# Retention followed by a gated feed-forward on one core: the sums of w_out as ScalarE negations plus accumulating transfers from GpSimd

## The chip, the cores and the metric

The kernel runs on one core of a Trainium2 chip. The metric is device time in microseconds; lower is better. The time before is 667.25 us, the median of three runs (667.02 to 668.68). The profiled execution took 667.05 us, of which 665.3 us are the span that the profile shows. TensorE's granted clock was 0.999 of full speed.

The engines are named as in the profile: PE is TensorE's matmuls and PEld its weight loads, DVE is VectorE, ACT is ScalarE, POOL is GpSimd, SP is SyncE, from whose queue the kernel's transfers start.

## The reference

```python
# retention: q, k, v are (4, 8, 768, 64)
for t in range(S):
    state = gamma[None, :, None, None] * state + np.einsum('bhd,bhe->bhde', k[:, :, t], v[:, :, t])
    y[:, :, t] = scale * np.einsum('bhd,bhde->bhe', q[:, :, t], state)
# to (3072, 512) tokens x, then the feed-forward; w_in is (512, 2048), w_out (2048, 512)
h = x @ w_in
sp = np.maximum(h, 0.0) + np.log1p(np.exp(-np.abs(h)))     # softplus
g = h * erf(sp)
return (g @ w_out).astype(np.float32)
```

The retention part produces the tokens 128 at a time (a chunk `j`); the feed-forward, which is nearly all of TensorE's work, consumes them.

## The kernel before

**Tokens and groups.** The first 512 tokens go through the feed-forward with plain matrix products, in groups 0 to 3 of 512 hidden features each (`hidden`, `project`). From group `G0` = 4 on, a group is 256 tokens times one half `s` of the hidden features (1024 of them); group 4 is half 0 of tokens 512 to 767, group 5 half 1 of the same tokens, group 6 half 0 of the next 256 tokens, and so on to group 23. "The first later group" of the change is group 5.

**Products from sums.** From group 4 on, the second product of the feed-forward is computed in 2x2 blocks with seven block products instead of eight, by a Strassen-Winograd scheme (`PRODUCTS`, `project_part`). It needs four sums of w_out blocks for each half: `T1 = 12 - 11`, `T2 = 22 - T1`, `T4 = 21 - T2`, `T3 = 22 - 12`, where "11", "12", "21", "22" are blocks of w_out. They are made once in the kernel by `sums(s)` and stay in `w_out_sb`; T3 is written over block "12", which the plain products of groups 0 and 1 must have read. Products 1, 2 and 3 need a plain block of w_out, 4 needs T4, 5 needs T1, 6 needs T2 and 7 needs T3. The first product (`hidden_steps`) uses a larger scheme of 26 steps on 4x4 blocks, with 30 sums of w_in for each half (`W_SUMS`, made by `sum_in(s, upto)`), from group 5 on. Group 4 still makes its hidden values with eight plain products (`hidden_plain`), since w_in's sums for half 0 overwrite plain blocks that group 4 uses.

**Order.** The order on each engine is written out by hand: a statement's place in the Python text is its place in its engine's queue, and each engine works its queue strictly in order. Generators are used to place small pieces: `next(last_steps)` emits the next sum of w_out (first the four of half 0, then the four of half 1), `w_sums` one sum of w_in of half 0, `e_sums` one sum of gated activations, `next_chunk` one step of the preparation of the next chunk of q and k. The dictionary `order` tells after which of the 26 hidden steps which of these are placed.

**A later group `g`.** In turn: 26 hidden steps, each one product into PSUM (L950) and one or two evictions, by DVE (L962, adding into h) or, for the first write to a block of h, by ScalarE (L964, L966); among them, at steps 14, 18 and 24, the products 1, 2 and 4 of the group before (L1033). Then ScalarE's softplus (L816), the retention visit (`sub_visit`), ScalarE's erf (L829), and the products 5, 6, 7 and 3 of the group before. DVE then multiplies h with erf (`gated`, L848). After an odd group DVE also makes the sums of the tokens for the next two groups (`x_sums`, L932). The hidden steps need w_in's sums, and the products 4 to 7 need the sums of w_out for the half of the group before.

**Where the sums stand before.** In group 4: 30 sums of w_in for half 1 on DVE, the four sums of w_out for half 0 (two before `project(3, 0)`, two after erf), then 8 sums of w_in for half 0. In group 5: the other 22 sums of w_in for half 0 (two each after steps 1 to 4, nine among steps 14 to 24, five after the visit). In group 6: three sums of w_out for half 1, after steps 12, 15 and 22, and the fourth after the visit.

**PSUM buffers of group 4.** Each of the eight plain products of `hidden_plain` goes into one of two "hp" buffers and is copied out by ScalarE (L982), so product n + 2 waits for copy n.

**Transfers.** All large transfers of this part start from SP: per chunk 256 KB each of k and v, 16 + 16 small ones of 16 KB for q and k in blocks (`load`), and the stores of the output, 256 KB each. GpSimd's queue is empty after the constants at the start.

Of the kernel before, what the change touches and what calls it, by code (L numbers as in the profile page):

```python
# [15 lines left out]
AF = mybir.ActivationFunctionType  # L16
ALU = mybir.AluOpType
# [28 lines left out]
W_SUMS = (  # L46
    (16, 2, 6, "+"),
    (17, 8, 10, "-"),
    (4, 4, 17, "+"),
    (10, 10, 16, "+"),  # L50
    (18, 16, 4, "-"),
    (19, 18, 5, "-"),
    (20, 1, 19, "-"),
    (20, 0, 20, "+"),
# [82 lines left out]
def kernel(  # L137
# [13 lines left out]
    nc = tc.nc  # L151
# [73 lines left out]
    def w_in_of(ft, kk):  # L225
        half, s, i = ft // (2 * FG), ft % (2 * FG) // FG, ft % FG
        return w_in_sb[:, s, 4 * (2 * half + i // 2) + kk, i % 2 * P : (i % 2 + 1) * P]
# [112 lines left out]
    def sum_in(s, upto):  # L340

        assert all(("hidden", 2 * FG + s * FG + u) in done for u in range(FG))
        for to, a, b, sign in W_SUMS[in_sums[s] : upto]:
            nc.vector.tensor_tensor(w_in_sb[:, s, to], w_in_sb[:, s, a], w_in_sb[:, s, b], op=OP[sign])
        in_sums[s] = max(in_sums[s], upto)

    def sums(s):

        assert ("project", s) in done
        x = {name: w_out_sb[:, s, at] for name, at in OUT.items()}  # L350
        for to, a, b in (("T1", "12", "11"), ("T2", "22", "T1"), ("T4", "21", "T2"), ("T3", "22", "12")):
            nc.vector.tensor_tensor(x[to], x[a], x[b], op=ALU.subtract)  # L352
            done.add((to, s))
            yield

# [15 lines left out]
    def later_sums():  # L371
        for s in range(2):
            yield from sums(s)

    weight_steps = weights()
    last_steps = later_sums()
# [155 lines left out]
    def prepared(j):  # L532

        if j >= NJ:
            return
        nc.vector.tensor_tensor(
            KQ[j][:, 0], KQ[j][:, 0],
            kq_s[:, j % NC, 0, :, None].to_broadcast([P, H, D]), op=ALU.mult,
        )
        yield  # L540
        blocks = (KB[j], KQ[j][:, 1].rearrange("p h d -> p (h d)"))
        for i, x in enumerate(blocks):
            x = x.rearrange("p (u a d) -> p u a d", u=HP, d=32)
            by = kq_b[:, j % NC, i, :, :, None].to_broadcast([P, HP, 4, 32])
            nc.vector.tensor_tensor(x, x, by, op=ALU.mult)
            yield
        for name, store, x in zip("kq", (KT, QT), blocks):
            store[j] = ret.tile([P, HP, C], F32, name=name + "T")
            nc.vector.transpose(store[j].rearrange("p u t -> p (u t)"), x)
            yield  # L550
# [156 lines left out]
    def sub_begin(j, pool=None):  # L707
        SC[j] = [ret_psum(pool) for _ in range(2)]
        sub_scores(j)
        sub_additions(j)  # L710
# [100 lines left out]
    def gate_softplus(g):  # L811


        name = "r" if g < 4 and g % 2 else "e"
        E[g] = act.tile([P, N], F32, name=name, bufs=1)
        nc.scalar.activation(E[g], HS[g], AF.Softplus)  # L816
# [28 lines left out]
    def gated(g, part=None):  # L845
        for a in range(2) if part is None else (part,):
            half = slice(a * N // 2, (a + 1) * N // 2)
            nc.vector.tensor_tensor(E[g][:, half], HS[g][:, half], E[g][:, half], op=ALU.mult)  # L848
            pace(-1.1)
# [61 lines left out]
    G0 = n_ft // FG  # L911
# [5 lines left out]
    def chunk_of(g):  # L917
        return TCH // SCH + (g - G0) // 2
# [51 lines left out]
    def hidden_plain(g):  # L970

        m, s = chunk_of(g), (g - G0) % 2
        HS[g] = act.tile([P, N], F32, name="h")
        h = HS[g].rearrange("p (f t u c) -> p f u t c", f=2, t=2, u=FG)
        x = XC[m // 2][:, :, m % 2 * SCH : (m % 2 + 1) * SCH]
        for f, u in itertools.product(range(2), range(FG)):
            to = ps_h.tile([P, TCH], F32, name="hp")[:, :SCH]
            for kk in range(n_k):
                nc.tensor.matmul(  # L979
                    to, w_in_of((2 * f + s) * FG + u, kk), x[:, kk], start=kk == 0, stop=kk == n_k - 1  # L980
                )
            nc.scalar.copy(h[:, f, u], to.rearrange("p (t c) -> p t c", t=2))  # L982
            yield
        done.update(("hidden", (2 * f + s) * FG + u) for f in range(2) for u in range(FG))
# [62 lines left out]
    def put_part(m, step):  # L1047


        o26, o57, o34, o1 = (O[m][i] for i in range(4))  # L1050
        if step == 0:
            R[m] = act.tile([P, 8, DH], F32, name="r", bufs=1)
            nc.scalar.copy(R[m][:, 7], o1[:, 0])
            return
        r = R[m]
        t0 = m * SCH
        if step == 1:
            nc.vector.tensor_tensor(
                r[:, 0:5:4], o26, r[:, 7:8].to_broadcast([P, 2, DH]), op=ALU.add
            )  # L1060
        elif step == 2:
            nc.vector.tensor_tensor(
                r[:, 5:7], o57, r[:, 4:5].to_broadcast([P, 2, DH]), op=ALU.add
            )
            nc.vector.tensor_tensor(r[:, 3], r[:, 6], o57[:, 0], op=ALU.add)
        else:
            nc.vector.tensor_tensor(r[:, 1:3], r[:, 5:7], o34, op=ALU.add)
            for t in range(2):
                nc.sync.dma_start(
                    out[t0 + t * P : t0 + (t + 1) * P, :],  # L1070
                    r[:, 2 * t : 2 * t + 2].rearrange("p a c -> p (a c)"),
                )
# [103 lines left out]
    def all_of(steps):  # L1176
        for _ in steps:
            pass
# [9 lines left out]
    load(j + 2)  # L1188
    gated(G0 - 1)
    for n, _ in enumerate(hidden_plain(G0), start=1):  # L1190
        if n == 3:
            sub_begin(j)
    sum_in(1, 20)
    x_sums(G0)
    sub_states(j)
    all_of(prepared(j + 1))
    next(last_steps)
    next(last_steps)
    sum_in(1, len(W_SUMS))
    project(G0 - 1, 0)  # L1200
    nc.scalar.activation(idle, idle, AF.Softplus)
# [3 lines left out]
    put_first(0)  # L1205
    gate_erf(G0)
    next(last_steps)
    next(last_steps)
    for tt in range(1, TT):
        project(G0 - 1, tt)  # L1210
        put_first(tt)
    gated(G0)
    sum_in(0, 8)
    j += 1

    def sums_left():
        for n in range(9, len(W_SUMS) + 1):
            sum_in(0, n)
            yield

    w_sums = sums_left()
    put = None
    for g in range(G0 + 1, NG):
        even = (g - G0) % 2 == 0
        more = j < NJ
        if put is not None:
            put_part(put, 0)
        e_sums = g_sums(g - 1)
        next(e_sums)
        next_chunk = prepared(j + 1) if even or put is None else iter(())  # L1230

        if put is not None:
            order = {18: (e_sums,), 20: (e_sums,), 24: (e_sums, e_sums)}
        else:
            order = {
                10: (next_chunk,), 14: (next_chunk, e_sums), 16: (next_chunk, e_sums),
                18: (next_chunk, e_sums), 20: (e_sums,), 24: (next_chunk,),
            }
        if g == G0 + 1:
            order.update({n: (w_sums,) * 2 for n in (1, 2, 3, 4)})  # L1240
            order[14] += (w_sums, w_sums)
            order[16] += (w_sums,)
            order[18] += (w_sums, w_sums)
            order[20] += (w_sums, w_sums)
            order[24] += (e_sums, w_sums, w_sums)
        elif g == G0 + 2:
            order.update({n: (last_steps,) for n in (12, 15, 22)})
        for n, _ in enumerate(hidden_steps(g), start=1):
            if put is not None and n in (14, 16, 18):
                put_part(put, n // 2 - 6)  # L1250
            for steps in order.get(n, ()):
                next(steps, None)
            if n in (14, 18, 24):
                project_part(g - 1, {14: 1, 18: 2, 24: 4}[n])
        put = None
        all_of(e_sums)
        all_of(next_chunk)

        nc.scalar.activation(idle, idle, AF.Softplus)
        gate_softplus(g)  # L1260
        if more:
            sub_visit(j, g)
        all_of(w_sums)
        if g == G0 + 2:
            all_of(last_steps)
        if g + 1 < NG and not even:
            x_sums(g + 1)
        if more:
            if even:
                all_of(prepared(j + 2))  # L1270
            if j + 3 < NJ:
                load(j + 3)
            j += 1
        gate_erf(g)
        for p in (5, 6, 7, 3):
            project_part(g - 1, p)
        if even:
            put = chunk_of(g - 1)
        if g == NG - 1:
            last_gated(g)  # L1280
        else:
            gated(g)

    g, m = NG - 1, chunk_of(NG - 1)
# [57 lines left out]
```

## Time and profile before

| engine | busy us | share of the span | instructions |
|---|---|---|---|
| PE | 657.3 | 99% | 6200 |
| PEld | 557.2 | 84% | 6200 |
| DVE | 517.0 | 78% | 1109 |
| ACT | 272.4 | 41% | 394 |
| POOL | 4.6 | 1% | 21 |

The costs of what the change touches, from the groups of the trace:

| what | line, engine | count | us each |
|---|---|---|---|
| sum of w_out, 128x1024 f32 | L352, DVE | 8 | 1.22 |
| sum of w_in, 128x256 f32 | L344, DVE | 60 | 0.42 |
| copy of a plain hidden product, 128x256 | L982, ACT | 8 | 0.37 |
| softplus or erf, 128x2048 | L816, L829, ACT | 22 + 21 | 1.91 |
| loading of an activation table | ACT | several a group | 1.28 |

How to read it: a share of busy time is a mean over the whole span. PE at 99% has few idle places, and a change that moves work between other engines can save only what PE idles there; so the table tells what moves, and the stretches of the trace, group by group, tell where it matters. An instruction's "idle before" with a releaser names the engine whose signal ended the wait. ACT's idle time of 128 us before softplus, for example, ends with DVE's last eviction and is only the rhythm of the groups.

The trace places group 4's plain products at 127.67 to 142.9 us, group 5's first hidden step at 158.48 and group 6's at 185.14.

### The profile page before, as it was taken

The numbers are of one execution on the slowest core, as the hardware profiler recorded it, in microseconds if no ns is written. First come the engines' busy times: TensorE is split into PE (matmuls) and PEld (weight loads), VectorE is DVE, ScalarE is ACT, GpSimd is POOL, SyncE is SP. The second block draws the span as 40 slices with busy tenths as digits, with TensorE's granted clock in tenths as the row PEclk, the third lists the DMA queues.
The fourth block names the chain that finished last, engine by engine and source line by source line (L and its number), as shares of the span: only waits on it lengthen the run. The fifth ranks groups of instructions, "written<-read, shape, count | busy, mean of one in ns | idle before, by whom it ended". The sixth has DMA issues, their size and how long they took to land.

```text
span 665.3 us, 15218 instructions
## 1 busy us (share of the span) xinstructions
PE 657.3 (99%) x6200; PEld 557.2 (84%) x6200; DVE 517.0 (78%) x1109; ACT 272.4 (41%) x394; POOL 4.6 (1%) x21
## 2 busy tenths in 40 slices
PE   8999999999999999999999999999999999999998
PEld 7744444576888999999999999999999999999997
DVE  5999999988997788678678678777787688476464
ACT  3468364344424244244244343442442542533440
POOL 1000000100000000000000000000000000000000
PEclk9999999999999999999999999999999999999999
DMA  9999944333421222222322322231232210000000
GB/s 188 222 241 216 236 133 106 63 62 61 116 41 32 66 49 45 70 42 48 73 40 46 73 41 45 36 77 34 47 79 36 43 55 1 2 33 0 1 33 32
DMA packets 158261, 47.68 MB, mean 72 GB/s; under 512 B 143088, under 2 KB 149616, under 8 KB 158192
## 3 DMA queue, kind: packets, MB, share of 16 engines
q1 hardware_dynamic: 157776, 46.72, 32.5%
q8 instruction: 48, 0.79, 0.5%
q14 instruction: 21, 0.17, 0.1%
q10 hardware_dynamic: 416, 0.01, 0.0%
HBM read 40.39 MB, written 6.29 MB: 70 GB/s over the span
## 4 chain that ended last, share of the span: by engine, by line
PE 95%; DVE 3%; DMA 1%; issue 1%; SPq 0%; ACT 0%; DVEq 0%
PE o L1033 36%; PE hp L950 21%; PE r L950 11%; PE hp L859 8%; PE o L895 8%; PE hp L979 2%; PE r L735 2%; PE hp L627 1%; PE o L771 1%; DVE h L962 1%; DMA kq<-in_k_dram 1%; PE r L556 1%; PE o L603 1%; PE r L750 1%; PE hp L750 1%
## 5 line engine op out<-in xcount | busy, mean ns | idle before, releaser
L1033 PE MATMUL o<-w_out_sb,h 128*128 128x256 f32 (+1 forms) x648 | 143.8, 379 | 0.4 <-DVE r L1297 0.4
L950 PE MATMUL hp<-xs,w_in_sb 128*128 128x128 f32 x988 | 138.9, 275 | 0.6 <-DVE h L962 0.6
L1033 PEld LDWEIGHTS o<-w_out_sb,h 128*128 128x128 f32 x648 | 120.5, 190 | 17.1 <-DVE r L1297 0.6
L950 PEld LDWEIGHTS hp<-xs,w_in_sb 128*128 128x128 f32 x988 | 128.3, 192 | 4.7 <-DVE h L962 1.8
L962 DVE TENSOR_TENSOR h<-h,hp 128x256 f32<-128x256 f32 x190 | 77.7, 418 | 67.5 <-PE hp L950 62.8
L1033 PE MATMUL o<-w_out_sb,e 128*128 128x256 f32 x480 | 113.6, 380 | 1.6 <-DVE w_out_sb L352 1.6
L1033 PEld LDWEIGHTS o<-w_out_sb,e 128*128 128x128 f32 x480 | 86.8, 190 | 11.2 <-DVE w_out_sb L352 1.8
L816 ACT ACTIVATE e<-h 128x2048 f32<-128x2048 f32 x22 | 42.0, 1911 | 128.0 <-DVE h L962 128.0
L962 DVE TENSOR_TENSOR h<-h,r 128x256 f32<-128x256 f32 x152 | 56.9, 415 | 21.6 <-PE r L950 20.7
L964 ACT COPY h<-hp 128x256 f32<-128x256 f32 x38 | 14.1, 372 | 132.7 <-PE hp L950 116.6
L950 PE MATMUL r<-xs,w_in_sb 128*128 128x128 f32 x456 | 63.3, 275 | 0.0
L950 PEld LDWEIGHTS r<-xs,w_in_sb 128*128 128x128 f32 x456 | 57.0, 192 | 0.0
L859 PE MATMUL hp<-xT,w_in_sb 128*128 128x512 f32 (+2 forms) x144 | 56.5, 548 | 0.0
L848 DVE TENSOR_TENSOR e<-h,e 128x1024 f32<-128x1024 f32 x42 | 49.3, 1214 | 9.2 <-ACT e L829 9.2
L859 PEld LDWEIGHTS hp<-xT,w_in_sb 128*128 128x128 f32 x144 | 25.8, 190 | 27.0 <-issue 24.6
L950 PE MATMUL hp<-xT,w_in_sb 128*128 128x128 f32 x304 | 46.3, 275 | 0.0
L950 PEld LDWEIGHTS hp<-xT,w_in_sb 128*128 128x128 f32 x304 | 41.5, 192 | 1.4 <-issue 0.5
L829 ACT ACTIVATE e<-e 128x2048 f32<-128x2048 f32 (+1 forms) x23 | 42.1, 1836 | 0.2
L966 ACT ACTIVATE h<-hp 128x256 f32<-128x256 f32 x57 | 21.8, 383 | 29.8 <-PE hp L950 28.5
L950 PE MATMUL r<-xT,w_in_sb 128*128 128x128 f32 x228 | 31.7, 275 | 0.0
L829 ACT ACT_TABLE_LOAD x24 | 30.8, 1283 | 0.4
L950 PEld LDWEIGHTS r<-xT,w_in_sb 128*128 128x128 f32 x228 | 28.5, 192 | 0.0
(159 smaller groups left out, 789.8 us busy)
## 6 DMA issues: line engine op xcount, KB each, us to landing
w_out_sb<-in_moe_w_out_dram SPq DMA_DIRECT2D x14, 512.0 KB, 6.6
kq<-in_k_dram SPq DMA_DIRECT2D x23, 256.0 KB, 4.0
v<-in_v_dram SPq DMA_DIRECT2D x23, 256.0 KB, 3.2
out_dram<-r SPq DMA_DIRECT2D x23, 256.0 KB, 2.6
kq<-in_q_dram SPq DMA_DIRECT2D x288, 16.0 KB, 1.8
kb<-in_k_dram SPq DMA_DIRECT2D x288, 16.0 KB, 1.7
w_in_sb<-in_moe_w_in_dram SPq DMA_DIRECT2D x8, 512.0 KB, 12.6
w_in_sb<-in_moe_w_in_dram SPq DMA_DIRECT2D x8, 256.0 KB, 8.0
```

Of the source, the lines that this page charges most:

```text
L735: nc.tensor.matmul(pp[r][col * D : (col + 1) * D, u % 2, t], x[own, u, :], QT[j][own, u, t], start=first(r, col), stop=True, skip_group_ch ...
L750: nc.tensor.matmul(other[a][own, u % 2, D:] if crossed else pp[a][own, u % 2, t], V[j][t, 2 * u + r, :], AM[j][t, r, u, :D], start=crossed ...
L816: nc.scalar.activation(E[g], HS[g], AF.Softplus)
L829: nc.scalar.activation(E[g][:, half], E[g][:, half], AF.Erf)
L848: nc.vector.tensor_tensor(E[g][:, half], HS[g][:, half], E[g][:, half], op=ALU.mult)
L859: nc.tensor.matmul(HP_[ft][:, t], w_in_of(ft, kk), XC[0][:, kk, t], start=(kk == 0), stop=(kk == n_k - 1),)
L895: nc.tensor.matmul(O[0][tt].rearrange("p (d c) -> p d c", d=2), E[g][:, u * TCH + tt * P : u * TCH + (tt + 1) * P], w_out_of(ft), start=(f ...
L950: nc.tensor.matmul(to[:, u, :], w_in_sb[:, s, w, u * P : (u + 1) * P], XS[m](x), start=first and u == 0, stop=True, skip_group_check=True,)
L962: nc.vector.tensor_tensor(h, h, of, op=ALU.add if plus else ALU.subtract)
L964: nc.scalar.copy(h, of)
L966: nc.scalar.activation(h, of, AF.Copy, scale=-1.0)
L1033: nc.tensor.matmul(O[m][i][:, half, at], G[g][a][:, u * P : (u + 1) * P], w_out_sb[:, s, OUT[b], u, at], start=i not in started, stop=(s = ...
```

## The change

Each sum of w_out is made in two parts instead of one DVE instruction: ScalarE writes the negated second operand to the sum's place (an activation Copy with scale -1), and a transfer from GpSimd's queue adds the first operand to it while it writes (128 partitions x 4 KB, 512 KB). The order of the four becomes T1, T2, T3, T4. T2 is computed from T1 and T4 from T2, so ScalarE's negation of T1 waits for T1's transfer, and that of T2 for T2's. T3 is negated in place over block "12", so after T1's transfer has read it.

The places change as well. Half 0: T1, T2 and T3 after plain products 1, 4 and 7 of group 4, T4 after erf of group 4. Half 1: T1, T2 and T3 after hidden steps 11, 17 and 23 of group 5, T4 after the visit of group 5, ahead of its erf; none is left in group 6. Of w_in's sums for half 0, 12 now stand before gating in group 4 and 8 after it (8 after it before), and 10 are left for group 5 (one each after steps 1 to 4, 14, 16, 18, 20 and 24, and one after the visit). The aim is to take work off DVE in the groups around the switch to the sums.

```diff
-        for to, a, b in (("T1", "12", "11"), ("T2", "22", "T1"), ("T4", "21", "T2"), ("T3", "22", "12")):
-            nc.vector.tensor_tensor(x[to], x[a], x[b], op=ALU.subtract)
+        for to, a, b in (("T1", "12", "11"), ("T2", "22", "T1"), ("T3", "22", "12"), ("T4", "21", "T2")):
+            nc.scalar.activation(x[to], x[b], AF.Copy, scale=-1.0)
+            nc.gpsimd.dma_start(x[to], x[a], accum_op=ALU.add)
             done.add((to, s))
             yield
...
     for n, _ in enumerate(hidden_plain(G0), start=1):
+        if n in (1, 4, 7):
+            next(last_steps)
         if n == 3:
             sub_begin(j)
     sum_in(1, 20)
     x_sums(G0)
     sub_states(j)
     all_of(prepared(j + 1))
-    next(last_steps)
-    next(last_steps)
     sum_in(1, len(W_SUMS))
     project(G0 - 1, 0)
...
     gate_erf(G0)
     next(last_steps)
-    next(last_steps)
+    sum_in(0, 12)
     for tt in range(1, TT):
         project(G0 - 1, tt)
         put_first(tt)
     gated(G0)
-    sum_in(0, 8)
+    sum_in(0, 20)
     j += 1
 
     def sums_left():
-        for n in range(9, len(W_SUMS) + 1):
+        for n in range(21, len(W_SUMS) + 1):
...
         if g == G0 + 1:
-            order.update({n: (w_sums,) * 2 for n in (1, 2, 3, 4)})
-            order[14] += (w_sums, w_sums)
-            order[16] += (w_sums,)
-            order[18] += (w_sums, w_sums)
-            order[20] += (w_sums, w_sums)
-            order[24] += (e_sums, w_sums, w_sums)
-        elif g == G0 + 2:
-            order.update({n: (last_steps,) for n in (12, 15, 22)})
+            order.update({n: (w_sums,) for n in (1, 2, 3, 4)})
+            for n in (14, 16, 18, 20, 24):
+                order[n] += (w_sums,)
+            order.update({n: (last_steps,) for n in (11, 17, 23)})
...
         all_of(w_sums)
-        if g == G0 + 2:
+        if g == G0 + 1:
             all_of(last_steps)
```

## The prediction

> **What bounds the kernel now.** I read the page first (busy shares, then the chain that ended last), then the tile and line of the sums that the change moves, then a table of stretches around the groups it touches, then the waits inside one of them.
>
> The shares and the head of the chain:
>
> ```profile
> PE 657.3 (99%) x6200; PEld 557.2 (84%) x6200; DVE 517.0 (78%) x1109; ACT 272.4 (41%) x394; POOL 4.6 (1%) x21
> ...
> PE 95%; DVE 3%; DMA 1%; issue 1%; SPq 0%; ACT 0%; DVEq 0%
> ```
>
> TensorE is the bound; only the places where it stands still can be won. The change touches DVE, ACT and POOL, so I looked for TensorE's idle time in the groups concerned. In the next view each line is one stretch: its bounds, its length, then busy time per engine. I cut from the first to the last matmul of the seven-product steps (L950, with the three L1033 products placed among them) of groups 5, 6, 7 and 8, and between these the 32 matmuls of the products 5, 6, 7, 3:
>
> ```profile
> 127.67:158.48 30.81, 30.81 (x242) 20.81 (x241) 26.53 (x64) 11.72 (x19) 0.00 (x0) 1.00 0.35 64
> 158.48:178.20 19.72, 19.34 (x258) 18.16 (x256) 17.93 (x46) 6.20 (x12) 0.00 (x0) 1.00 0.40 92
> 178.20:185.14 6.94, 6.94 (x33) 6.11 (x34) 6.35 (x25) 4.42 (x5) 0.00 (x0) 1.00 0.35 66
> 185.14:207.13 21.99, 20.16 (x258) 18.38 (x256) 19.01 (x38) 5.97 (x11) 0.00 (x0) 1.00 0.15 28
> 207.13:214.07 6.94, 6.94 (x33) 6.12 (x33) 6.78 (x13) 4.42 (x6) 0.00 (x0) 1.00 0.33 63
> 214.07:233.05 18.98, 18.98 (x258) 18.17 (x256) 13.34 (x29) 5.97 (x11) 0.00 (x0) 1.00 0.26 62
> ...
> 240.00:258.97 18.97, 18.97 (x258) 18.16 (x256) 13.78 (x30) 5.97 (x11) 0.00 (x0) 1.00 0.17 32
> ```
>
> The same 258 matmuls take 18.98 us in groups 7 and 8, where DVE is busy for 13.3 to 13.8, but 19.72 in group 5 (DVE 17.9) and 21.99 in group 6 (DVE 19.0). So **0.74 us in group 5 and 3.01 us in group 6** are lost because DVE is late; group 4 (the first line) has no idle TensorE at all. The waits inside group 6 name the cause, the w_out sums of L352, and that line's own answer gives their length:
>
> ```profile
> PEld o L1033 <- DVE w_out_sb L352: 1.8, 1, 1.8
> PE o L1033 <- DVE w_out_sb L352: 1.6, 1, 1.6
> PEld hp L950 <- DVE h L962: 1.0, 3, 0.4
> ...
> L352 DVE TENSOR_TENSOR w_out_sb<-w_out_sb x8: 1182/1216/1224, 140.0 to 208.7; 128x1024 f32<-128x1024 f32 x8
> ```
>
> The product 4 waited 1.6 us for its T4, the third such sum; the rest of the 3.01 us is small waits for evictions queued on DVE behind the sums.
>
> **What the Trainium skill says.** "DMA: Bandwidth & Descriptors", section "SWDGE vs HWDGE vs iDMA": accumulating in a transfer goes only by GpSimd's software path. Its section "Anatomy of one DMA — SWDGE (gpsimd) path" prices a transfer of that path at 2.0 us + bytes/436e3; for 512 KB that is 3.2 us, and its "Rules for kernel authors" say that an accumulate reads its destination and writes it later, so a second stream is read. The trace of before has no such transfer. "SBUF — State Buffer", section "Who interferes with whom": DVE's tensor_tensor with both inputs in SBUF takes GpSimd's read interface only, and descriptor generation needs the write interface (inferred, by that page), so DVE's sums should not starve it. No run here shows that yet. ScalarE's price needs no page; the trace has the shape:
>
> ```profile
> L314 ACT ACTIVATE w_out_sb<-w_out_sb,below 128x1024 uint32<-128x1024 uint32 x7 | 8.0, 1149 | 8.1 <-DVE w_out_sb L313 8.1
> L829 ACT ACTIVATE e<-e 128x1024 f32<-128x1024 f32 x2 | 2.0, 1049 | 0.0
> ```
>
> **The change part by part.**
>
> DVE loses eight L352 sums, 8 x 1.216 = 9.7 us. Four lay in group 4, where TensorE has no idle time: worth nothing. Three lay inside group 6's stretch (3 x 1.22 = 3.65 us) and one right after it. Without them group 6's DVE time falls from 19.0 to 15.4. Further, DVE enters group 6 earlier: of the 5 w_in sums before the sums of x one remains, 4 x 0.41 = 1.6 us, so gating of group 5 (2.35 us at 186.04) falls earlier by that much and part of it leaves the stretch: about 13.8, which is group 8's load, and group 8 has no idle. **Gain 3.0 us.**
>
> The w_in sums of half 0: before, 8 in group 4 and 22 in group 5; now 20 and 10. In group 4 DVE starts them at 149.15, where the w_out sums stood: 12 x 0.387 = 4.65 us to 153.8, ScalarE's erf having ended at 152.6; gating 2.36 to 156.2; 8 + 4 more sums, 4.65 us, to 160.8. The first eviction on DVE started at 161.03 before, so nothing is late: cost nothing, hidden behind the 24 matmuls of L895 (10.6 us) and the first steps that ScalarE evicts. In group 5 four sums fewer stand among steps 14 to 24 (9 before, 5 now): 4 x 0.41 = 1.6 us off an engine that made TensorE lose 0.74. **Gain 0.7 us.**
>
> ScalarE gains eight negations of 128x1024. I take 1.05 us each (the f32 row; the other row is 1.15). Eight are 8.4 us on an engine busy for 41%. Three stand between the copies of group 4's plain product; a copy takes 0.37 and comes every 1.72 us, so 1.42 fits. One stands after erf of group 4, before copies that wait up to 2.9 us for TensorE. The other four are in group 5. By duration alone they cost nothing.
>
> The waits are the new thing. T2 is computed from T1, T4 from T2, so ScalarE's negation for T2 waits until T1's transfer has landed, and what follows on ScalarE's queue waits too. Call **L** the time from the end of a negation to the landing of its transfer, as seen by a waiting engine.
> - Group 4, half 0. T1's negation ends at 129.97 + 1.05 = 131.0. T2's stands behind the fourth copy (ends at 136.43). Copy 5 must begin by 138.8, since step 7 begins at 139.2 in the buffer that copy 5 frees (two buffers). So T1 must land by 137.8: **L up to 6.8 costs nothing**, each further us costs one.
> - Group 5, half 1. T1's negation follows the copy that ends at 163.52, and ends at 164.57. T2's ends at 165.62 + L (for L over 3.3), T3's one later, then ScalarE loads the softplus table for 176.2: in time up to L = 8. T2's sum lands at 165.62 + 2L. T4's negation waits for that, behind the copies to xT that end at 178.7; behind it stand the erf table (1.28) and erf (1.91), and for erf waits DVE's gating, free for it at 183.7. 183.7 - 1.91 - 1.28 - 1.05 = 179.5, so **L up to 6.9 costs nothing**; beyond, erf slips by 2 us for each us. Some 1.6 us of slip are free, because before gating ended 3.25 us into group 6 and the first TensorE wait there came only after the L352 sum at 191.8.
> - TensorE's matmuls of products 4 to 7 now wait for transfers. Half 0's last (T4, negated by 153.7) lands near 160 and is first read at 173.3; half 1's lands near 186 and is read at 199. Nothing.
>
> How long is L? Lower end: 3.2 us, the page's price. With the second stream read at the same rate (1.2 us more) 4.4. Upper end: 512 KB loads of w_out took 6.6 us in the trace, at a time when the engines were 90% busy; with 1.2 us for a second read 7.8, and a slow adder could make it 10. The engines are 20 to 40% busy around 131 to 138 and 163 to 173, mostly with 16 KB loads, and a 256 KB store lands in 3.4 us there. I take **L = 5.5 us**, under both limits.
>
> Other loads: the accumulating transfers share the engines with the kb loads of group 4, for which DVE idled 0.76 us at 137.5. A further us there is hidden, as DVE has 2.4 us less to do before its mask at 147.96.
>
> Sum: 667.25 - 3.0 - 0.7 = **663.5 us**. The rest of the span (the groups after 6, at 18.98 or less with TensorE full, and the head) does not change.
>
> **The rivals.**
> 1. *The transfer's latency takes the place of the sums.* At L = 10: group 4 loses 10 - 6.8 = 3.2; group 5's erf slips 2 x 3.1 = 6.2, less 1.6 free, 4.6. So 663.5 + 3.2 + 4.6 = **671.3 us**, slower. For it: two limits within 1.5 us of my L, an unseen transfer kind, ScalarE strictly in order. Against it: the 3.4 us stores and the page's 3.2 us. It breaks even near L = 8.6.
> 2. *Half of it comes.* L between 7 and 8.5, or DVE starving descriptor generation now and then (DVE is busy for 4.97 of the 5 us from 163 to 168). At L = 8: 1.2 + 0.6 = 1.8 lost, **665.3 us**; near 8.5 no change.
> 3. *DVE stays late in group 6 because gating and the sums of x bind it, not L352.* Then only the 1.6 us wait goes: **665.6 us**. Against it: groups 7 and 8 have gating too and no idle.
>
> **How the numbers follow.** Forecast 0.68, slow transfer 0.18, rivals 2 and 3 together 0.14 (half of these gain over 2.0 us, which is 0.3%; most of the rest are within it). Faster 0.73, within 0.3% 0.09, slower 0.18. The range starts at 662.9 (all 3.75 us, and a little drift) and reaches over rivals 2 and 3 into the weakest third of rival 1: 668.5. Inside are 0.68 + 0.14 + 0.05.
>
> **What would show it.** Right: group 6's 258 matmuls in 19.0 us and group 5's in under 19.2, no TensorE wait on DVE's w_out_sb, no idle TensorE in group 4, ScalarE waiting under 1 us for w_out_sb's transfers at the second negation of group 4. Wrong: ScalarE's copies L982 late behind a wait for a transfer; erf of group 5 ending after 184.5; transfers over 7 us from issue to landing.

## The result, and the profile after

The changed kernel takes **663.28 us**, the median of four runs (663.08 to 663.55), against 667.36 us for the kernel before, measured beside it. The ratio is 0.9936, with a 95% interval of 0.9918 to 0.9953. Measured again beside two of the experiments it was 663.14 us, ratio 0.9930 (0.9918 to 0.9942). The forecast was 663.5 us. About a third of the runs of the kernel before, and fewer or none of most others, take 1.5 to 2 us longer than the rest, so a ratio and the medians shown beside it can differ by up to 0.2%.

The page of the changed kernel begins its shares and its chain like this (busy time and share of each engine, then the share of each engine in the chain that ended last):

```profile
PE 655.3 (99%) x6200; PEld 556.6 (84%) x6200; DVE 508.4 (77%) x1101; ACT 280.1 (42%) x402; POOL 11.5 (2%) x29
...
PE 98%; DMA 1%; DVE 0%; SPq 0%; ACT 0%; issue 0%
```

DVE lost 8.6 us and ACT gained 7.7; that alone says nothing about the time. The line to read is the chain's: DVE had 3% of it and now has none, and TensorE went from 95 to 98%.

The table of stretches, cut at the same events as before (bounds, length, then busy time of PE, PEld, DVE, ACT and POOL, granted clock, DMA share, GB/s); in order: group 4, the hidden steps of group 5, its products, the hidden steps of group 6, and those of group 7:

```profile
127.50:158.32 30.82, 30.82 (x241) 20.80 (x240) 25.13 (x70) 15.54 (x23) 3.59 (x4) 1.00 0.62 113
158.32:177.23 18.91, 18.91 (x257) 18.10 (x255) 16.14 (x40) 9.34 (x15) 2.56 (x3) 1.00 0.66 122
177.23:184.24 7.01, 7.01 (x38) 6.19 (x33) 6.71 (x25) 5.20 (x6) 0.85 (x1) 1.00 0.95 183
184.24:203.16 18.92, 18.92 (x258) 18.11 (x256) 14.08 (x31) 5.91 (x11) 0.00 (x0) 1.00 0.43 91
...
210.10:229.08 18.98, 18.98 (x259) 18.15 (x257) 12.47 (x29) 5.91 (x11) 0.00 (x0) 1.00 0.28 65
```

Group 5 fell from 19.72 to 18.91 us and group 6 from 21.99 to 18.92; both are now as short as group 7. Together that is 3.88 us, and the span fell by 665.3 - 661.5 = 3.8. Group 4 is as long as before (30.82 against 30.81).

The new parts, line by line: the negations, GpSimd's instructions that start the transfers, and the time from the issue of a transfer to its landing:

```profile
L352 ACT ACTIVATE w_out_sb<-w_out_sb x8: 1041/1058/1072, 129.7 to 178.2; 128x1024 f32<-128x1024 f32 x8
...
L353 POOL DMA_DIRECT2D w_out_sb<-w_out_sb x8: 850/854/1007, 131.1 to 179.5; - x8
...
DMA to landing us min/median/max: 4.6/5.2/7.0
```

A negation takes 1.06 us, GpSimd is busy for 0.85 us with each transfer, and half of the transfers land within 5.2 us; the slowest of the eight took 7.0. The order of time on ScalarE in group 4 shows the wait that mattered (start, length, what, and in brackets the idle time and what ended it):

```profile
129.71 1.06 ACT L352 ACTIVATE w_out_sb<-w_out_sb 128x1024 f32<-128x1024 f32 x1
...
135.91 0.37 ACT L983 COPY h<-hp 128x256 f32<-128x256 f32 x1 [2.64 <-PE hp L980]
136.68 1.06 ACT L352 ACTIVATE w_out_sb<-w_out_sb 128x1024 f32<-128x1024 f32 x1 [0.40 <-DMA w_out_sb<-w_out_sb]
137.64 0.36 ACT L983 COPY h<-hp 128x256 f32<-128x256 f32 x1
```

T1's negation ended at 130.77 and T2's could start at 136.68: L was 5.9 us, and ScalarE waited 0.40 us for it. (L is the prediction's name for the time from the end of a negation to the landing of its transfer, as a waiting engine sees it.) In group 5 the same interval was 164.32 to 170.44, 6.1 us; ScalarE waited 2.68 us there with nothing behind it that was due.

### The profile page after: what moved, and what is told of

It is laid out like the page before. It is cut to its first block, busy times and chain, and to the rows that moved or that the text cites. A ratio compares the mean times of both kernels' runs of the same rounds, so it can differ in the third digit from the quotient of the medians.

```text
span 661.5 us, 15245 instructions
## 1 busy us (share of the span) xinstructions
PE 655.3 (99%) x6200; PEld 556.6 (84%) x6200; DVE 508.4 (77%) x1101; ACT 280.1 (42%) x402; POOL 11.5 (2%) x29
## 4 chain that ended last, share of the span: by engine, by line
PE 98%; DMA 1%; DVE 0%; SPq 0%; ACT 0%; issue 0%
PE o L1034 37%; PE hp L951 22%; PE r L951 12%; PE hp L860 8%; PE o L896 8%; PE hp L980 2%; PE r L736 2%; PE hp L628 1%; PE o L772 1%; DMA kq<-in_k_dram 1%; PE r L557 1%; PE o L604 1%; PE r L751 1%; PE hp L751 1%; PE r L524 1%; PE r L772 0%
```

## The experiments

There were twelve runs; eight are in this table, and e4 to e7 have their figures further down. Lengths of the hidden steps of groups 5 and 6 are cut from each trace between the same two matmuls, with DVE's busy time in them:

| kernel | ratio to before (95%) | median us | group 5 us (DVE) | group 6 us (DVE) |
|---|---|---|---|---|
| before | 1 | 667.36 | 19.72 (17.9) | 21.99 (19.0) |
| changed | 0.9936 (0.9918 to 0.9953) | 663.28 | 18.91 (16.1) | 18.92 (14.1) |
| e1_dve_new_places | 0.9989 (0.9980 to 0.9997) | 666.94 | 22.25 (20.6) | 18.95 (15.2) |
| e2_win_old | 0.9951 (0.9938 to 0.9963) | 664.43 | 19.65 (17.9) | 19.08 (15.9) |
| e3_win_only | 1.0011 (1.0001 to 1.0021) | 668.01 | 20.35 (18.3) | 21.87 (17.2) |
| e8_half1_only | 0.9938 (0.9927 to 0.9950) | 663.83 | 19.20 (17.3) | 18.91 (14.1) |
| e9_half1_dve_early6 | 0.9945 (0.9933 to 0.9957) | 664.19 | 18.91 (16.2) | 19.56 (17.2) |
| e10_dve_only_early6 | 0.9953 (0.9938 to 0.9968) | 664.69 | 19.20 (17.3) | 19.56 (17.2) |
| e11_changed_again | 0.9930 (0.9918 to 0.9942) | 663.14 | | |
| e12_place_alone | 0.9986 (0.9979 to 0.9993) | 666.51 | 19.66 (17.9) | 21.37 (19.0) |

e9, e10 and e11 shared one chip, where the kernel before had a median of 667.64 us; beside the other experiments it had 667.15 to 667.31.

### The parts of the change

**e1_dve_new_places**: the places of the change, the old instruction.

```diff
-            nc.scalar.activation(x[to], x[b], AF.Copy, scale=-1.0)
-            nc.gpsimd.dma_start(x[to], x[a], accum_op=ALU.add)
+            nc.vector.tensor_tensor(x[to], x[a], x[b], op=ALU.subtract)
```

> All of the change but the mechanism: the eight sums of w_out are DVE subtractions again, at the changed places. My theory (the gain is DVE time taken out of groups 5 and 6): DVE gets 3 x 1.22 us back among group 5's steps and 1.22 after its visit, and starts group 5 about 1.1 us late because T4 of half 0 stands ahead of the w_in sums; group 5's hidden stretch then needs about 16.1 + 3.7 + 1.1 = 20.9 us of DVE and grows from 18.9 to 20.5 to 21.5 us; group 6 stays near 19. Total 665.0 to 666.0. Rival (only the place in group 6 mattered, not the engine): 663.3.

Measured 666.94 us, above the 665.0 to 666.0 expected. Group 6 is at 18.95 us as forecast, but group 5 lost more than forecast: 22.25 us, although DVE's busy time in it, 20.6 us, is near the 20.9 that the forecast was made from. TensorE's waits from group 4 on, in this kernel (who waited for whom, total, times, longest):

```profile
PE hp L950 <- DVE h L962: 1.7, 2, 1.1
PE r L950 <- DVE h L962: 0.3, 1, 0.3
```

The evictions queue behind the sums on DVE. So these places alone only move the loss from group 6 to group 5; the rival's 663.3 is ruled out.

**e2_win_old**: the mechanism and its places, w_in's sums as before.

```diff
-    sum_in(0, 12)
...
-    sum_in(0, 20)
+    sum_in(0, 8)
...
-            order.update({n: (w_sums,) for n in (1, 2, 3, 4)})
+            order.update({n: (w_sums,) * 2 for n in (1, 2, 3, 4)})
...
```

> The mechanism and its places kept, the w_in sums of half 0 back where they were (8 in group 4, 22 in group 5). My theory: group 5 keeps its 0.74 us of lost time (19.7 us), group 6 is at 19.0 to 19.2 us: 664.0 to 664.3. Rival (the w_in sums are what made group 6 late, through the five after the visit): group 6 loses 1 us or more, 665.0 or above.

Measured 664.43 us. Group 5 keeps its loss (19.65 us) and group 6 is at 19.08. So the new instruction at its new places is worth about 3 us with no help from the w_in sums. The move of these is worth 664.43 - 663.28 = 1.15 us on top by the medians, and 0.9 us by the lengths of the two groups. The new instruction at the old places was not tried.

**e3_win_only**: the kernel before, with only the w_in sums moved.

```diff
     next(last_steps)
     next(last_steps)
+    sum_in(0, 12)
...
-    sum_in(0, 8)
+    sum_in(0, 20)
...
-        for n in range(9, len(W_SUMS) + 1):
+        for n in range(21, len(W_SUMS) + 1):
...
```

> The kernel before with only the w_in sums of half 0 moved; w_out sums on DVE at the old places. My theory: group 5 falls to about 19 us (0.7 gained, less up to 0.5 because DVE starts it behind two w_out sums and twelve more w_in sums in group 4), group 6 starts with DVE 1.6 us earlier and loses about 1.5 us instead of 3.0: 665.0 to 666.0. Rival (DVE is late in group 6 because of gating and the sums of x, not of L352): group 6 falls to 19 us and the whole gain comes, 663.5.

Measured 668.01 us, ratio 1.0011 (1.0001 to 1.0021): slightly slower than before, where both theories had a gain. Both of my steps for it failed. From the order of time in this kernel: DVE and TensorE around the start of group 5, then DVE's first evictions of group 6, whose first matmul is at 185.69, and TensorE's wait for T4:

```profile
158.32 4.47 DVE L344 TENSOR_TENSOR w_in_sb<-w_in_sb 128x256 f32<-128x256 f32 x12
162.71 0.41 DVE L962 TENSOR_TENSOR h<-h,hp 128x256 f32<-128x256 f32 x1
...
163.18 1.16 PE L950 MATMUL hp<-xs,w_in_sb 128*128 128x128 f32 x8 [1.11 <-DVE h L962]
...
188.19 0.42 DVE L962 TENSOR_TENSOR h<-h,hp 128x256 f32<-128x256 f32 x1 [1.09 <-PE hp L950]
189.53 0.42 DVE L962 TENSOR_TENSOR h<-h,r 128x256 f32<-128x256 f32 x1 [0.92 <-PE r L950]
...
202.72 1.99 PE L1033 MATMUL o<-w_out_sb,e 128*128 128x256 f32 x8 [1.57 <-DVE w_out_sb L352]
```

With half 0's w_out sums still on DVE, the added w_in sums end at 162.8 instead of 160.5 as in the changed kernel, and group 5's first DVE eviction is late: TensorE waits 1.1 us for it, and the group takes 0.6 us more than before where 0.7 less was forecast. And group 6 is no shorter although DVE entered it earlier: the early start was spent in two waits of about 1 us for TensorE's first steps, and T4's sum still stood two steps ahead of the product that reads it, a wait of 1.57 us as before the change.

**e8_half1_only**: half 0's sums on DVE again, at the changed places.

```diff
+            if s == 0:
+                nc.vector.tensor_tensor(x[to], x[a], x[b], op=ALU.subtract)
+            else:
...
```

> The change, but with the four w_out sums of half 0 as DVE subtractions at the changed places in group 4; half 1 by negation and transfer. My theory (half 0's part is worth nothing by itself, TensorE had no idle time there): DVE starts group 5's evictions about 1.1 us later, group 5 had 2.8 us of idle DVE: 663.3 to 663.9. Rival (group 4 has no room for 4.9 us of w_out sums beside the twelve added w_in sums): group 5's stretch grows by 1 us or more, 664.5 or above.

Measured 663.83 us: within the forecast, 0.55 us above the changed kernel by the medians. The ratios, 0.9938 and 0.9936, show no difference; the trace shows 0.3 us, in group 5 at 19.20. So half 0's transfers can be left out at a cost of some tenths of a us. The likely cause is the one w_out sum that now stands ahead of w_in's sums in group 4: DVE's first eviction of group 5 starts at 161.73 us instead of 160.82.

### The latency of the transfer as a wait

**e4_t2_early**: T2 of half 0 after plain product 2 instead of 4.

```diff
-        if n in (1, 4, 7):
+        if n in (1, 2, 7):
```

> The changed kernel with T2 of half 0 placed after plain product 2 of group 4 instead of 4. ScalarE then waits for T1's transfer with copies 3 and 4 behind it. My theory (limit of the latency: copy 3 must begin before step 5 does): the negation ends near 137.7, copy 3 begins there instead of 132.9, step 5 stands still from 135.7 to 138.1: TensorE loses about 2.4 us, total 665.7. Rival (PSUM buffers or later slack take up a late copy, or only DVE matters here): 663.3.

Measured 665.74 us. The order of time in this kernel, ScalarE and then TensorE:

```profile
136.40 1.06 ACT L352 ACTIVATE w_out_sb<-w_out_sb 128x1024 f32<-128x1024 f32 x1 [4.99 <-DMA w_out_sb<-w_out_sb]
137.36 0.63 ACT L983 COPY h<-hp 128x256 f32<-128x256 f32 x2
...
137.77 7.17 PE L980 MATMUL hp<-xT,w_in_sb 128*128 128x256 f32 x32 [2.03 <-ACT h L983]
```

ScalarE waits 4.99 us, the copies 3 and 4 go out together at 137.36, and TensorE starts again at 137.77 after 2.03 us (2.4 on its weight loads), close to the 2.4 forecast. So a late landing does stop TensorE through the two PSUM buffers: rival 1's mechanism exists. The prediction's own limit, 6.8 us for T2 after product 4, was worked out in the same way; against it the changed kernel, with L at 5.9, has 0.9 us of latency left. No run went past that limit itself.

**e7_half1_late**: half 1's first three sums later in group 5.

```diff
-            order.update({n: (last_steps,) for n in (11, 17, 23)})
+            for n in (18, 21, 23):
+                order[n] = order.get(n, ()) + (last_steps,)
```

> The changed kernel with half 1's T1, T2, T3 after steps 18, 21, 23 of group 5 instead of 11, 17, 23. On ScalarE the first negation then stands behind the copy of step 16 (ends 167.8) instead of that of step 10 (163.4). My theory: T1 lands at about 175, softplus starts near 178.5 instead of 175.8, the copies to xT, the sums of x, erf and gating slip by 2.7 to 3.5 us; 1 to 2 us of this are free; TensorE loses 0.5 to 2 us at the start of group 6: 664.0 to 665.3. Rival (ScalarE has 58% of idle time, so such a wait is free): 663.3.

Measured 663.43 us, ratio 0.9929 (0.9909 to 0.9949): by the median no loss beside the changed kernel. But the execution with the trace was the slowest of the four, 664.37 us; the others took 663.17 to 663.51. ScalarE, DVE and TensorE of that execution in order of time:

```profile
173.80 2.00 ACT L352 ACTIVATE w_out_sb<-w_out_sb 128x1024 f32<-128x1024 f32 x2 [4.95 <-DMA w_out_sb<-w_out_sb]
...
181.71 1.06 ACT L352 ACTIVATE w_out_sb<-w_out_sb 128x1024 f32<-128x1024 f32 x1 [2.05 <-DMA w_out_sb<-w_out_sb]
...
184.38 0.61 PE L951 MATMUL hp<-xT,w_in_sb 128*128 128x128 f32 x4
186.02 2.36 DVE L849 TENSOR_TENSOR e<-h,e 128x1024 f32<-128x1024 f32 x2 [1.25 <-ACT e L830]
...
188.76 1.16 PE L951 MATMUL hp<-xs,w_in_sb 128*128 128x128 f32 x8 [0.41 <-DVE h L963]
```

and from its chain of what waited for what, T2's transfer, and the 32 matmuls that follow group 6's hidden steps:

```profile
175.15 6.53 DMA w_out_sb<-w_out_sb
...
204.27 7.10 PE o L1034 x32
```

T1 landed 4.9 us after its negation instead of the 6 I had assumed, so softplus began at 177.2 and not 178.5. But T2 took 6.5 us from issue to landing, and T4's negation, with erf behind it, waited 2.05 us for it. Gating began 2.7 us later than in the changed kernel (186.02 against 183.31) and ended at 188.4, 4 us into group 6. Group 6's hidden steps, cut as in the table, took 19.8 us, 0.9 more than in the changed kernel; 0.41 of that is TensorE's wait in the lines above, the rest smaller losses around it. So in this execution the forecast came true: 0.5 to 2 us lost, 664.0 to 665.3 in total, and a slip of 2.7 us that cost 0.9 leaves about 1.8 us free, close to the prediction's 1.6. Why the other three lost next to nothing is open, as they left no trace; an earlier landing of T2 would do it.

**e5_plain**: plain transfers, one run; the addition is left out.

```diff
-            nc.gpsimd.dma_start(x[to], x[a], accum_op=ALU.add)
+            nc.gpsimd.dma_start(x[to], x[a])
```

> The changed kernel with plain transfers of the first operand in place of accumulating ones; the sums of w_out are left out, so its output is not the reference's. It prices the accumulation alone. My theory (the destination is read as a second stream, 1.2 us more of 512 KB): median landing 4.0 to 4.4 us instead of 5.2, total unchanged at 663.3. Rival (the price is in the software path and its fixed part): 5.0 to 5.3.

Time 663.84 us; a single run can't tell this from 663.3. The landing times of L353's transfers in this kernel, and the line of their queue from 125 to 190 us (packets, MB, share of the 16 engines):

```profile
DMA to landing us min/median/max: 3.0/3.5/4.8
...
q0 software_dynamic: 1152, 4.19, 17.9%
```

and the same line in the changed kernel:

```profile
q0 software_dynamic: 1152, 4.19, 34.0%
```

The packets and bytes counted are the same, but in the changed kernel the engines are occupied for twice as long, and a transfer lands 1.7 us later (5.2 against 3.5). So the accumulation has a price of its own, larger than the 1.2 us expected, and the 3.5 us lie below the 4.0 to 4.4 of my theory. That a second stream is read is not shown by this, only that adding costs time. GpSimd's own time for one also fell, from 0.85 to 0.53 us.

### GpSimd as the adder

**e6_gpsimd_tt**: subtraction by GpSimd.

```diff
-            nc.scalar.activation(x[to], x[b], AF.Copy, scale=-1.0)
-            nc.gpsimd.dma_start(x[to], x[a], accum_op=ALU.add)
+            nc.gpsimd.tensor_tensor(x[to], x[a], x[b], op=ALU.subtract)
```

> The changed kernel with the sums of w_out as GpSimd subtractions instead of a negation and a transfer. Nothing but data holds GpSimd back, so it makes most of them early, around 117 to 140 us. From the small GpSimd operations of the trace (128x8 0.294, 128x32 0.327 us) one takes an estimated 1.7 us, eight 14 us. My theory, after the Trainium skill's page SBUF (Who interferes with whom: DVE with two SBUF inputs and a GpSimd operation that reads SBUF exclude each other): DVE, busy for over 80% there, is late by several us, its subtractions of 128x256 take longer than 0.42 us, and the total is 665 to 672. Rival (no exclusion that shows): 663.3, and this way would be simpler than the transfers.

Measured 675.09 us, ratio 1.0100 (1.0077 to 1.0123). GpSimd's and DVE's lines in order of time, in this kernel, and TensorE's longest wait:

```profile
121.00 20.25 POOL L352 TENSOR_TENSOR w_out_sb<-w_out_sb 128x1024 f32<-128x1024 f32 x8
...
118.89 17.42 DVE L344 TENSOR_TENSOR w_in_sb<-w_in_sb 128x256 f32<-128x256 f32 x12
136.23 2.82 DVE L536 TENSOR_TENSOR kq<-kq,kq_s 128x512 f32<-128x512 f32 x1
...
PE r L627 <- DVE qT L549: 8.9, 1, 8.9
```

and the same twelve sums of DVE in the kernel before:

```profile
117.74 4.98 DVE L344 TENSOR_TENSOR w_in_sb<-w_in_sb 128x256 f32<-128x256 f32 x12
```

While GpSimd subtracts, a DVE sum takes 17.42/12 = 1.45 us instead of 0.42, and the scaling of kq 2.82 instead of 0.69; after 141 us, when GpSimd is done, DVE is back at 0.68. The q and k of the next chunk come so late that TensorE stands for 8.9 us. That is not the whole loss of 11.8 us against the changed kernel: the granted clock of TensorE in this trace was 0.50 from 139 to 147 us, and the 40 plain matmuls after the wait took 9.71 us instead of 8.90. The same sums by transfer leave DVE alone. In the changed kernel GpSimd issued T2's transfer while DVE was idle and T3's while DVE made ten w_in sums:

```profile
138.04 0.87 POOL L353 DMA_DIRECT2D w_out_sb<-w_out_sb  x1 [5.96 <-ACT h L983]
142.71 0.86 POOL L353 DMA_DIRECT2D w_out_sb<-w_out_sb  x1 [3.79 <-ACT w_out_sb L352]
```

It took as long beside the busy DVE as beside the idle one, and the ten sums took 3.90 us, against 3.93 in the kernel before.

### Place or load

e3 left open why group 6 stayed long. **e9_half1_dve_early6** is the changed kernel with half 1's sums back on DVE, early in group 6; **e10_dve_only_early6** has half 0's on DVE as well, at the changed places in group 4; **e11_changed_again** is the changed kernel beside them; **e12_place_alone** makes only this edit in the kernel before:

```diff
         elif g == G0 + 2:
-            order.update({n: (last_steps,) for n in (12, 15, 22)})
+            for n in (1, 5, 8):
+                order[n] = order.get(n, ()) + (last_steps,)
```

> The changed kernel, but half 1's w_out sums are DVE subtractions in group 6, early: T1 after step 1, T2 after step 5, T4 after step 8, T3 after the visit (before: T1, T2, T4 after steps 12, 15, 22). It tells the place of DVE's sums from their load, which is the same as before. Place theory (group 6 lost its 3 us because the sums stood among the bunched evictions and T4 two steps ahead of its product): they fall into 2 us of idle DVE at the start of group 6, which then takes 18.9 to 19.4 us; total 663.3 to 664.0. Load theory (the theory of the prediction: DVE has too much to do in group 6): group 6 takes 20.5 us or more, total 665.0 or above.

> As the run with half 1 on DVE early in group 6, and half 0's four sums on DVE as well, in group 4: no negation and no transfer at all, the w_in sums moved as in the change. Half 0 on DVE cost 0.5 us when tried alone. Place theory: 663.8 to 664.5, so the order would give nearly all that the new mechanism gives. Load theory: 665.5 or above.

> The changed kernel unaltered, measured beside the two others on the same chip: 663.3 by all theories.

> The kernel before with one edit: half 1's w_out sums stand on DVE after steps 1, 5, 8 of group 6 (and T3 after the visit) instead of 12, 15, 22. The w_in sums stay as before, so DVE enters group 6 1.6 us later than in the other early runs and has no idle time at its start. Place theory in its strong form (only T4's sum close ahead of its product cost much): group 6 takes 19.5 to 20.2 us instead of 22.0, total 665.0 to 665.8. If the move of the w_in sums is needed to make the room: group 6 takes 21 us or more, total 666.3 or above.

e9 took 664.19, e10 664.69, e11 663.14 and e12 666.51 us; e9 and e10 lie 0.2 us above their place forecasts and well under the load ones. Put e3 beside e9 and e10 in the table: **DVE is busy for 17.2 us in group 6 in all three, yet the group takes 21.87 us in e3 and 19.56 in the others**. So the load alone does not decide; at this load the place of three sums makes 2.3 us. In e9 (order of time, DVE, then TensorE's only wait):

```profile
183.54 2.35 DVE L854 TENSOR_TENSOR e<-h,e 128x1024 f32<-128x1024 f32 x2
185.81 1.22 DVE L355 TENSOR_TENSOR w_out_sb<-w_out_sb 128x1024 f32<-128x1024 f32 x1
186.98 0.42 DVE L968 TENSOR_TENSOR h<-h,hp 128x256 f32<-128x256 f32 x1
187.32 1.22 DVE L355 TENSOR_TENSOR w_out_sb<-w_out_sb 128x1024 f32<-128x1024 f32 x1
...
190.38 1.16 PE L956 MATMUL hp<-xs,w_in_sb 128*128 128x128 f32 x8 [0.39 <-DVE h L968]
```

The sums fill the gaps in which DVE waited for TensorE in e3, and one wait of 0.39 us is left; the group is 0.6 us longer than in the changed kernel. In e12 the same place finds no gap, since the five w_in sums still stand ahead of gating:

```profile
186.09 2.35 DVE L848 TENSOR_TENSOR e<-h,e 128x1024 f32<-128x1024 f32 x2
188.36 1.22 DVE L352 TENSOR_TENSOR w_out_sb<-w_out_sb 128x1024 f32<-128x1024 f32 x1
...
189.97 1.16 PE L950 MATMUL hp<-xs,w_in_sb 128*128 128x128 f32 x8 [1.05 <-DVE h L962]
...
192.90 1.16 PE L950 MATMUL hp<-xs,w_in_sb 128*128 128x128 f32 x8 [0.75 <-DVE h L962]
```

Group 6 is at 21.37 us. Moving the w_in sums alone (e3) loses 0.1%, moving half 1's sums alone (e12) wins 0.14% (0.07 to 0.21), and both with no new mechanism, with half 0's sums at the changed places too (e10), win 0.47% (0.32 to 0.62). In group 6 the one makes the gap and the other uses it. The changed kernel wins 0.70% beside e10. By the lengths of groups 5 and 6 together, 41.71 us before, 38.76 in e10 and 37.83 in the changed kernel, order alone gives 2.95 of the 3.88 us, and the negations and transfers add 0.93. No kernel tried was clearly faster than the changed one.

## Why the prediction was right, point by point

- **Where the time lay** (0.74 us in group 5, 3.01 in group 6): right. They fell by 0.81 and 3.07 us, 3.88 together, and the span fell by 3.8.
- **DVE's load in group 6 after the change**, forecast about 13.8 us: 14.08. **Group 4 without loss**: right, 30.82 us. The load was a good guide here, but it is not what sets the time: e2 has 15.9 us of DVE in group 6 and hardly any loss, while e3 and e9 have the same 17.2 and differ by 2.3 us. The prediction's waits told more than its loads: T4's sum stood just ahead of its product, and evictions queued behind the other sums.
- **L = 5.5 us and the limits of 6.8 and 6.9**: L was 5.9 and 6.1 at the two places that wait, under both limits. The 5.5 was a choice between bounds of 4.4 and 7.8, so its closeness is partly luck. e4 shows the wait behind the limit of group 4 near its forecast size. For group 5, e7's trace bears out the free slip behind gating: about 1.8 us against the 1.6 put down. No run had an L above the limits at the change's own places.
- **The price of the accumulation**: the lower end had 1.2 us for a second stream; e5 shows 1.7.
- **Gating 1.6 us earlier as a help in group 6**: this step failed as a step by itself. e3 has it and group 6 stayed at 21.87 us. It helps only together with sums that stand where the gap is (e9 against e12). In the changed kernel it was hardly needed: e2, without it, has group 6 at 19.08 us instead of 18.92.
- **Half 0's sums worth nothing**: nearly. e8 puts them at 0.3 us by the trace and 0.55 by the medians.
- **The move of the w_in sums worth 0.7 us**: 1.15 us by e2's median, 0.9 by the lengths of groups 5 and 6 (19.65 + 19.08 against 18.91 + 18.92).
- **The kb load**: it did come later, as DVE waited 3.0 us for it in group 4 instead of 0.8, and it was hidden behind the mask's wait for TensorE, as argued.
- **The page on DVE and GpSimd** ("SBUF — State Buffer" of the Trainium skill, section "Who interferes with whom"): both halves agree with the runs. GpSimd issued a transfer in 0.86 us beside DVE's sums and in 0.87 beside an idle DVE, and its own operations that read SBUF made DVE's two-input sums 3.5 times as long (e6).

Rival 1's chain of waits is real, but its latency was not reached. Of rival 2 there is one faint sign: the slowest of the eight transfers took 7.0 us to land, the edge of what the prediction called a sign of being wrong, but ScalarE's only two waits for these transfers were for others. Rival 3 is ruled out, since gating and the sums of x stayed and groups 5 and 6 have no idle TensorE.

## What to carry to other kernels

Before blaming an engine's load for a late stage, compare two orders with the same load: here three long helper instructions cost about 3 us where they stood just ahead of a consumer and among bunched evictions, and 0.6 us where they fell into gaps. A chain that goes through transfers needs the landing time between its links, so work out what is queued behind each waiting instruction and by when its buffer is due; here, by the prediction's limit, 0.9 us of latency more would have begun to cost. An idle engine is not a free helper where its work slows the busy one, as GpSimd's subtractions slowed DVE: look at the busy engine's durations while both run.

## What the runs showed that I had not expected

Accumulating 512 KB inside the SBUF occupied the transfer engines for twice the share of a plain transfer (34.0% against 17.9% of the same stretch) and took 1.7 us longer to land. GpSimd's subtraction of 128x1024 took 2.53 us beside a busy DVE, where I had estimated 1.7. Landing times spread from 4.6 to 7.0 us in one execution of the changed kernel and to 9.1 in that of e7, so a wait that costs nothing at the median can cost time in a single execution, as in e7's traced one.
